# Strided heads as 18-token classes on four partition quarters, q and k cast in natural order, strided V cast in place, first two batches turned by TensorE

## The chip, the cores and the metric

The kernel runs on one core of one Trainium2 chip. The metric is device time in microseconds (us), from runs of the whole kernel; inputs and outputs lie in HBM. Engines are named as the profile names them: PE (TensorE; PEld its weight loads), DVE (VectorE), ACT (ScalarE), POOL (GpSimd), SP (SyncE). POOL and SP issue DMAs here; SPq in a row is an instruction that issues one on SP's hardware queue.

## The reference, cut to what matters

q, k and v are float32 [8 batches, 8 heads, 576 tokens, 64]. Heads 0 to 3 are local (a token sees itself and the 31 before it), heads 4 to 7 strided (a token sees the tokens before it, and itself, whose position has the same remainder by 32: 18 tokens for each of 32 remainders, a "class").

```python
    scores = scale * np.matmul(q, k.transpose(0, 1, 3, 2))
    mask_local = (rel >= 0) & (rel < stride)
    mask_strided = (rel >= 0) & (pos[None, :] % stride == pos[:, None] % stride)
...
    attn = attn / (np.sum(attn, axis=-1, keepdims=True) + 1e-09)
    return np.matmul(attn, v).astype(np.float32)
...
    h = x @ w_in
    P = a[0] + a[1] * h + a[2] * h2 + a[3] * h3
    Q = 1.0 + np.abs(b[0]) * np.abs(h) + np.abs(b[1]) * h2
    g = P / (Q + 1e-06)
    return (g @ w_out).astype(np.float32)
```

The attention output, tokens by 512 features (4608 rows), is x; w_in is 512 by 2048, w_out 2048 by 512, the output 4608 by 512 in float32.

## The kernel before, in words

All work is written as operations of a small planner (`Prog`). Each operation has an engine, an estimated duration, a key (its due time) and the tiles it reads and writes. `schedule` (L124) plays them through: on each engine the ready operation with the smallest key goes next. The result is one fixed order per engine, which the chip keeps; `emit` puts a semaphore wait ahead of each operation that needs one. So an operation that waits holds everything behind it on its engine, DMA issues on SP and POOL included. A DMA's estimate is a pair: the time that it takes of one common DMA resource, and a latency behind it (L185 to L188).

Per batch there are five steps.

1. `casts` (L419): POOL issues seven DMAs that read float32 from HBM and write bf16 back to HBM. Four of them (`local`, L428) interleave two local heads of q or k token by token, in runs of 64 elements (128 bytes), 1152 runs each; three (`bulk`, L436) copy strided q, strided k and all of v in natural order, in long runs.
2. `loads` (L463): SP issues four DMA transposes into SBUF (`lqT`, `lkT` L469; `sqT`, `skT` L475), each of 1152 rows of 128 elements (256 bytes); six DMAs for the local v tile `vL` (L481, L486: 4 x 64 x 17 + 2 x 64 = 4480 runs of 128 bytes), whose 32-token blocks lie on partitions twice over; eight DMAs for the strided v tile `vS` (L495: 8 x 36 x 16 = 4608 runs of 128 bytes).
3. `attention`: local scores in PSUM (L522, mask L509, row maximum on DVE L546, its subtraction by a matmul L553, exp on ACT L559 and L563), the probabilities turned by a DMA transpose (`ptL`, L566), their product with `vL` (L635), whose 65th column of ones gives the row sums, and a normalising multiply on DVE (`norm`, L655, L658). The strided heads go in two passes of two heads. Tokens are taken 36 at a time (remainder by 16, two classes in one; even and odd tokens on two partition halves), 64 products of 36 by 36 a batch (L591), with a mask that cuts the pairs apart; their probabilities are turned by two DMA transposes (`ptS`, L619), multiplied with `vS` (L687) and normalised.
4. The result is stored to HBM (`xs`; L665, L669, L696) and read back by DMA transposes into `xt`, features on partitions (`gather`, L711).
5. `mlp` works on chunks of 512 tokens (nine; chunk c can start when batch c is gathered, chunks 7 and 8 both need batch 7). In each, 16 blocks of four matmuls with `Win` (L731), a copy to bf16 on ACT (L735), then the rational function in two groups of 8 blocks: |h| on ACT (L746; for chunk 0 on DVE, L750), the denominator and the polynomial on DVE (L753, L755, L768 to L776), 1/Q as Ln and Exp on ACT (L759, L764). Then 64 matmuls with `Wout` (L789), four copies (L795) and four stores (L801).

The weights are cast into SBUF by four POOL DMAs between the casts of batches 0 and 1 and behind them. Casts of batch b+2 are tied to the first load of batch b+1. Attention of batch b has due times from `b*PER - 20`, gather `b*PER - 2`, its chunk `b*PER + 10`, with `PER` = 33.

## Time and profile before

| what | value |
|---|---|
| three timed runs | 584.54, 588.31, 590.23 us; median 588.31 us |
| profiled execution: span from first to last instruction | 586.6 us |
| busy: PE, DVE, ACT, POOL | 349.3, 314.7, 306.6, 61.5 us |
| mean granted TensorE clock | 0.903 of full speed |
| DMA packets, of which under 512 bytes | 213187, 196128 |
| first matmul with `Win` | at 152.61 us |

The span is that of one execution; the median of the timed runs is 1.7 us above it, and no separate time of the profiled execution is on the page. A row such as `L731 PE MATMUL ps<-xt,Win ... x554 | 149.1, 408 | 58.7 <-DMA xt<-xs 52.8` says: 554 matmuls of line 731, 149.1 us in which at least one of them ran, 408 ns from start to end of one (they overlap), and 58.7 us in which PE stood idle ahead of them, 52.8 of these until the DMA that fills `xt` had landed. In the rows of stretches the columns are length, busy time (and instructions) of PE, PEld, DVE, ACT and POOL, granted clock, the summed time of DMA packets as a share of 16 engines (over 1 where packets of two queues overlap), and GB/s.

### The profile page before, as it was taken

Reading aid. Unit: us, or ns where it says so; the run is one execution under the profiler, and the core shown is the slowest. Engines: PE = TensorE matmul, PEld = TensorE weight load, DVE = VectorE, ACT = ScalarE, POOL = GpSimd, SP = SyncE. Lnnn points to the kernel's source line nnn. Section 1 sums busy time; section 2 is a strip of 40 time slices with the busy share of each in tenths; the row PEclk is TensorE's granted clock in tenths of the full one; section 3 lists DMA queues with packets and bytes.
Section 4 is the critical chain, followed back from the end, with each engine's and each line's share of the span. In section 5 each row is a group of like instructions: output and inputs, shape, how many; then the busy total and the mean of one; then the engine's idle time right before and its main releaser. Section 6 shows DMA issues by size and latency. Waiting matters only on the chain.

```text
span 586.6 us, 7831 instructions
## 1 busy us (share of the span) xinstructions
PE 349.3 (60%) x3393; PEld 167.0 (28%) x3440; DVE 314.7 (54%) x227; ACT 306.6 (52%) x317; POOL 61.5 (10%) x64
## 2 busy tenths in 40 slices
PE   1012105103552379087796597994898899996846
...
DMA  9999999979999999979959995795214414000101
GB/s 127 182 163 121 91 114 172 73 145 174 82 133 185 61 153 165 87 114 181 127 86 200 115 100 123 142 103 127 46 45 97 71 39 115 19 36 18 54 19 72
DMA packets 213187, 62.71 MB, mean 107 GB/s; under 512 B 196128, under 2 KB 207008, under 8 KB 212640
## 3 DMA queue, kind: packets, MB, share of 16 engines
q1 hardware_dynamic: 171744, 43.84, 57.2%
q0 software_dynamic: 41408, 18.35, 27.8%
...
q14 instruction: 8, 0.07, 0.0%
HBM read 46.18 MB, written 28.31 MB: 127 GB/s over the span
## 4 chain that ended last, share of the span: by engine, by line
SPq 37%; PE 16%; DVE 16%; ACT 16%; DMA 12%; issue 4%; POOL 0%; ACTq 0%; POOLq 0%
SPq L495 10%; SPq L486 8%; PE ps L731 8%; PE ps L789 6%; DMA xt<-xs 5%; ACT z L746 5%; SPq L481 5%; DMA xs<-xS 4%; SPq L469 4%; SPq L475 4%; ACT h L735 4%; ACT u L759 3%; DVE u L755 3%; ACT u L764 2%; DVE z L770 2%
## 5 line engine op out<-in xcount | busy, mean ns | idle before, releaser
L731 PE MATMUL ps<-xt,Win 128*128 128x512 bf16 x554 | 149.1, 408 | 58.7 <-DMA xt<-xs 52.8
L789 PE MATMUL ps<-Wout,h 128*128 128x512 bf16 x553 | 149.9, 409 | 29.4 <-DVE h L776 17.0
L735 ACT ACTIVATE h<-ps 128x512 bf16<-128x512 f32 x144 | 82.0, 610 | 99.3 <-PE ps L731 98.4
L731 PEld LDWEIGHTS ps<-xt,Win 128*128 128x128 bf16 x576 | 56.3, 104 | 133.2 <-DMA xt<-xs 48.6
L789 PEld LDWEIGHTS ps<-Wout,h 128*128 128x128 bf16 x576 | 57.0, 104 | 101.5 <-DVE h L776 19.5
L759 ACT ACTIVATE u<-u,consts 128x2048 bf16<-128x2048 bf16 x36 | 70.6, 2000 | 19.3 <-DVE u L755 19.3
L764 ACT ACTIVATE u<-u 128x2048 bf16<-128x2048 bf16 x36 | 67.0, 1910 | 0.0
L428 POOL DMA_DIRECT2D lq<-in_q_dram x16 | 34.3, 2278 | 259.2 <-DMA lqT<-lq 258.4
L546 DVE TENSOR_REDUCE ng<-ps 128x18 bf16<-128x1152 f32 x8 | 10.8, 1356 | 93.5 <-PE ps L522 93.4
L746 ACT ACTIVATE z<-h 128x2048 bf16<-128x2048 bf16 x32 | 59.5, 1915 | 0.3
L522 PE MATMUL ps<-lkT,lqT 64*32 64x64 bf16 (+1 forms) x576 | 8.1, 207 | 79.6 <-DMA lkT<-lk 79.4
L753 DVE TENSOR_SCALAR u<-z,coef 128x4096 bf16<-128x4096 bf16 x18 | 24.1, 1338 | 58.2 <-ACT z L746 58.2
L559 ACT ACTIVATE pL<-ps 128x1024 bf16<-128x1024 f32 x8 | 8.2, 1019 | 79.9 <-PE ps L553 79.9
L776 DVE TENSOR_TENSOR h<-z,u 128x4096 bf16<-128x4096 bf16 x18 | 41.3, 2292 | 8.1 <-ACT u L764 7.6
L428 POOL DMA_DIRECT2D lk<-in_k_dram x16 | 41.6, 2923 | 0.0
L773 DVE TENSOR_TENSOR z<-z,h 128x4096 bf16<-128x4096 bf16 x18 | 41.2, 2291 | 0.5
L755 DVE TENSOR_TENSOR u<-u,z 128x4096 bf16<-128x4096 bf16 x18 | 41.1, 2283 | 0.4
L770 DVE TENSOR_TENSOR z<-z,h 128x4096 bf16<-128x4096 bf16 x18 | 40.9, 2272 | 0.3
L591 PE MATMUL ps<-skT,sqT 64*36 64x36 bf16 x512 | 20.2, 245 | 25.1 <-DMA skT<-sk 25.1
L795 ACT ACTIVATE os<-ps 128x512 f32<-128x512 f32 x36 | 21.5, 604 | 22.3 <-PE ps L789 22.2
L601 DVE TENSOR_REDUCE ng<-ps 100x16 bf16<-100x576 f32 x16 | 12.1, 755 | 35.8 <-PE ps L591 35.8
L522 PEld LDWEIGHTS ps<-lkT,lqT 64*32 64x32 bf16 x576 | 6.0, 94 | 86.9 <-DMA lkT<-lk 81.0
...
## 6 DMA issues: line engine op xcount, KB each, us to landing
...
```

What stands on the lines that cost most here:

```text
L428: P.op("pool", lambda e: e.dma_start(d_t[b, pair, :, :].rearrange("s (hh d) -> s hh d", hh=2), s_t[b, 2 * pair:2 * pair + 2, :, :].rearran ...
L486: P.op("sp", lambda e, hh=hh, pair=pair: e.dma_start(vl.t[64 * hh:64 * hh + 64, pair, 1:NB, 0:64], bass.AP(tensor=vs, offset=(b * H + 2 * ...
L495: P.op("sp", lambda e, r=r, h=h: e.dma_start(vS.t[64 * r:64 * r + CS, h, :, 0:64], bass.AP(tensor=vs, offset=(b * H + HL + h) * S * D, ap= ...
L731: r = e.matmul(bank(ph, 0, CH), Win[:, kk, f * 128:(f + 1) * 128], xt.t[:, kk, :], start=(kk == 0), stop=(kk == NK1 - 1))
L735: P.op("act", lambda e, f=f, ph=ph, h=h: e.activation(h.t[:, f % G, :], bank(ph, 0, CH), AF.Copy), 0.597, ky, r=[ph], w=[h], occ=0.494)
L746: P.op("act", lambda e, z=z, h=h, i=i: e.activation(z.t[:, half * i:half * i + half, :], h.t[:, half * i:half * i + half, :], AF.Abs), 1.9 ...
L755: dv(lambda e, z=z, u=u: e.tensor_tensor(u.t[:, :, :], u.t[:, :, :], z.t[:, :, :], op=Alu.mult), 2.28, 4, r=[z], m=[u])
L759: lns.append(P.op("act", lambda e, u=u, i=i: e.activation(u.t[:, half * i:half * i + half, :], u.t[:, half * i:half * i + half, :], AF.Ln, ...
L764: exs.append(P.op("act", lambda e, u=u, i=i: e.activation(u.t[:, half * i:half * i + half, :], u.t[:, half * i:half * i + half, :], AF.Exp ...
L770: dv(lambda e, z=z, h=h: e.tensor_tensor(z.t[:, :, :], z.t[:, :, :], h.t[:, :, :], op=Alu.mult), 2.28, 8, r=[h], m=[z])
L776: dv(lambda e, z=z, h=h, u=u: e.tensor_tensor(h.t[:, :, :], z.t[:, :, :], u.t[:, :, :], op=Alu.mult), 2.28, 14, r=[z, u], m=[h])
L789: r = e.matmul(bank(po, 0, Fout), groups[g].t[:, j, m * 128:(m + 1) * 128], Wout[:, kk, :], start=(kk == 0), stop=(kk == NF - 1))
```

## The change

Names stay; line numbers below are those of the changed file.

**Planner.** The DMA estimate has two queues, hardware (SP) and software (POOL), which share the engines; most durations and keys are new. Attention of batch b has due times from `b*35 - 26`, gather `b*35 - 8`, its chunk `b*35 + 10`. The rings of `xt` (2 to 3), `xl` and `xS` (1 to 2) grow, that of `h` shrinks (5 to 4 tiles).

**Casts.** No interleaving is left. For batches 2 to 7 there are five DMAs in long runs (local q and k, strided q and k, local v; 16 rows of 9216 elements each), into one HBM tensor `qk`. For batches 0 and 1, q and k go straight into SBUF (`sg`: 72 partitions with 8 tokens of each of 4 heads), and never through HBM. In every batch, strided v is cast straight into `vS` by four DMAs (18 partitions, runs of 512 elements), which takes its loads off SP.

```diff
-        local(0, q, lq, T_lq[b])
-        local(0, k, lk, T_lk[b])
-        local(1, q, lq, T_lq[b])
-        local(1, k, lk, T_lk[b])
-        bulk(q, sq, HL, HL, HL, T_sq[b])
-        bulk(k, sk, HL, HL, HL, T_sk[b])
-        bulk(v, vs, 0, H, H, T_v[b])
+            bulk(q, HL, qk, o + 2 * HS, T_qs[b])
+            bulk(k, HL, qk, o + 3 * HS, T_ks[b])
+            bulk(q, 0, qk, o, T_ql[b])
+            bulk(k, 0, qk, o + HS, T_kl[b])
+            bulk(v, 0, vs, b * HS, T_v[b])
+        t = R_vS.next()
+        for bq in range(4):
+            P.op("pool", lambda e, bq=bq, t=t: e.dma_start(
+                t.t[32 * bq:32 * bq + NI, :, :, :].rearrange("p h c d -> p h (c d)"),
+                bass.AP(tensor=v.tensor, offset=v.offset + (b * H + HL) * S * D + 8 * bq * D,
+                        ap=[[32 * D, NI], [S * D, HL], [1, 8 * D]])),
```

**Loads.** For batches 2 to 7, one DMA transpose brings strided q and k together (144 rows of 2048 elements, that is 2304 rows of 128), and one each local q and k (2304 rows of 128 elements that start 64 elements apart, so that a head lies on either partition half). `vL` is loaded once (4 DMAs, 2304 runs of 128 bytes) and its shifted second half copied inside SBUF (2 DMAs).

```diff
+            P.op("sp", lambda e, t=t: e.dma_start_transpose(
+                t.t[:, :, :], bass.AP(tensor=qk, offset=o + 2 * HS, ap=[[2048, 2 * HL * NI], [1, 2048]])),
+                1.4, key, r=[T_qs[b], T_ks[b]], w=[t], dma=(2.6, 2.0))
+            for nm, R, off, T in (("lq", R_lq, 0, [T_ql[b], T_kl[b]]), ("lk", R_lk, HS, [T_kl[b], T_qs[b]])):
...
+                    t.t[:, :], bass.AP(tensor=qk, offset=o + off, ap=[[D, HL * S], [1, 128]])),
+                    1.4, key + 0.1, r=T, w=[t], dma=(2.6, 2.0))
...
+            P.op("sp", lambda e, hh=hh: e.dma_start(
+                vl.t[64 * hh:64 * hh + 32, :, 1:NB, :], vl.t[64 * hh + 32:64 * hh + 64, :, 0:NB - 1, :]),
+                0.5, key + 0.3, r=[own], w=[vl], dma=(0.15, 2.0))
```

**Turning by PE.** For batches 0 and 1 PE transposes q and k (`turn_qk`, 128 small transposes, 8 copies shared by DVE and ACT), the probabilities (`turn`, 17 transposes, 4 copies), and the tokens of x that go into the batch's own chunk (`turn_x`, 24 transposes, 6 copies). Only their remaining 64 and 128 tokens go by `xs` and a gather. From batch 2 on the probabilities and x are turned by DMA as before, with one `ptS` transpose in the place of two.

**Strided heads.** 128 products of 18 by 18 a batch, four classes at a time on the four 32-partition quarters, all four heads in one pass: one mask (2 matmuls instead of 4), one maximum, one subtraction and one exp instead of two. The column of ones is gone from `vS`; row sums come from 8 matmuls with a 4-column block matrix `BO` and one reciprocal. The product with `vS` is 128 matmuls of 18 by 32 by 64 (L750), and two multiplies of 1024 columns stand for four DVE operations.

```diff
+                    for a in range(4):
+                        for p in range(2):
+                            c2 = 4 * bq + a
+                            r = e.matmul(bank(SS, 512 * p + NI * (4 * h + bq), NI, 32 * a, 32 * a + NI),
+                                         sqk.t[64 * p:64 * p + 64, c2, NI * h:NI * h + NI],
+                                         sqk.t[64 * p:64 * p + 64, c2, NI * (HL + h):NI * (HL + h) + NI],
+                                         start=False, stop=True, skip_group_check=True,
+                                         tile_position=(64 * p, 32 * a))
```

**MLP.** The groups are [4, 4, 8] blocks in chunk 0, [8, 4, 2, 2] in chunk 8, [8, 8] else. The second half of a chunk's `Wout` matmuls waits for its last group. Operations and their work are else the same.

```diff
+            sizes = [4, 4, 8] if nxt == 0 else [8, 4, 2, 2] if nxt == NCH - 1 else [8, 8]
+            mlp(nxt, nxt * PER + 10, sizes, [nxt > 0] * len(sizes))
```

**How the order moves.** First POOL, at the program's start. Before (`lq`, `lk`, `sq`, `sk`, `v` are HBM tensors):

```order
L428 DMA lq<-in_q_dram 1152x1x64
L428 DMA lk<-in_k_dram 1152x1x64
...
L436 DMA sq<-in_q_dram 16x9216
L436 DMA sk<-in_k_dram 16x9216
L436 DMA v<-in_v_dram 32x9216
L451 DMA Win<-in_moe_w_in_dram 128x4x1024 x2
```

Now (`sg` and `vS` lie in SBUF):

```order
L431 DMA v<-in_v_dram 16x9216
L441 DMA sg<-in_q_dram 72x4x512
L441 DMA sg<-in_k_dram 72x4x512
...
L454 DMA vS<-in_v_dram 18x4x512 x4
L464 DMA Win<-in_moe_w_in_dram 128x4x1024 x2
```

The two `L428` rows stand twice before, the two `L441` rows twice now: the first batch's nine DMAs stand ahead of `Win`, where seven stood.

Then PE, up to the first matmuls with `Win`. Before, the end of that stretch (batch 1's scores, then batch 0's local products, then chunk 0):

```order
L591 MATMUL ps<-skT,sqT 36x36 x64
L553 MATMUL ps<-ng,IDN 128x512 x2
L553 MATMUL ps<-ng,IDN 128x128
L608 MATMUL ps<-ng,IDN 100x288 x4
L635 MATMUL ps<-vL,ptL 32x65 x36
L731 MATMUL ps<-xt,Win 128x512 x36
L635 MATMUL ps<-vL,ptL 32x65 x36
L731 MATMUL ps<-xt,Win 128x512 x12
```

Now the same place (L571, L853 and L836 are transposes by PE; `sg` in L537 is batch 1's staged q and k):

```order
L571 MATMUL ps<-IDN,pL 128x128 x9
L734 MATMUL ps<-BO,ptS 128x4 x8
L750 MATMUL ps<-vS,ptS 32x64 x128
L783 MATMUL ps<-vL,ptL 32x65 x72
L853 MATMUL ps<-IDN,xS 128x128 x16
L836 MATMUL ps<-IDN,xl 128x128 x8
L889 MATMUL ps<-xt,Win 128x512 x16
L537 MATMUL ps<-IDN,sg 64x72 x128
```

Chunk 0 stands now behind one batch's attention instead of behind two batches' scores, and after its first 16 matmuls PE turns to batch 1's q and k.

Last SP, for one batch in the middle. Before (batch 2's loads, batch 0's gather between them):

```order
L469 DMA_TRANSPOSE lqT<-lq 128x2x576
L469 DMA_TRANSPOSE lkT<-lk 128x2x576
L475 DMA_TRANSPOSE sqT<-sq 128x4x288
L475 DMA_TRANSPOSE skT<-sk 128x4x288
L481 DMA vL<-v 32x2x64
L486 DMA vL<-v 64x17x64 x2
...
L711 DMA_TRANSPOSE xt<-xs 128x4x512
L711 DMA_TRANSPOSE xt<-xs 128x4x64
L495 DMA vS<-v 36x16x64 x8
L566 DMA_TRANSPOSE ptL<-pL 128x9x128
```

Now (batch 3's loads, with batch 2's stores and gather between them; two rows of `out_dram` stores left out):

```order
L485 DMA_TRANSPOSE sqkT<-qk 128x16x144
L765 DMA xs<-xS 72x2x256 x4
L491 DMA_TRANSPOSE lqT<-qk 128x2304
L491 DMA_TRANSPOSE lkT<-qk 128x2304
L500 DMA vL<-v 32x18x64 x4
...
L808 DMA xs<-xl 128x4x256
L817 DMA xs<-xl 64x128 x2
...
L514 DMA vL<-vL 32x2x1105 x2
L561 DMA_TRANSPOSE ptS<-pS 128x8x128
L870 DMA_TRANSPOSE xt<-xs 128x4x384
```

The eight `vS` rows are gone from SP, and batch 2's gather stands behind batch 3's `ptS`, which needs batch 3's scores.

More of the change, by code (lines that the diff above doesn't have):

```diff
@@ L623, in attention, with srcL, ssum @@
-        key += 14
+        def srcL():
+            return ppL.t
+        srcL.tile = ppL
+        turn(srcL, ptL, 9, key, 1.3)
+        T_xs[b].new()
+        t0 = b * S
+        key += 8
+        SB_ = Banks(1)
+        def ssum(e):
+            r = None
+            for g in range(8):
+                r = e.matmul(bank(SB_, 4 * g, 4), ptS.t[:, g, :], BO[:, :], start=True, stop=True, skip_group_check=True)
+            return r
+        P.op("pe", ssum, 8 * 0.07, key, r=[ptS, T_c], w=[SB_])
+        rcS = R_rc.next()
```

657 lines of the change are left out of this document (390 added, 267 removed).

## The prediction

> **What bounds the kernel now.** I read the page's slices first, then the stretches between gathers, then SP's queue, then the groups of instructions.
>
> ```profile
> PE   1012105103552379087796597994898899996846
> DMA  9999999979999999979959995795214414000101
> q1 hardware_dynamic: 171744, 43.84, 57.2%
> q0 software_dynamic: 41408, 18.35, 27.8%
> GB/s 127 182 163 121 91 114 172 73 145 174 82 133 185 61 153 165 87 114 181 127 86 200 115 100 123 142 103 127 46 45 97 71 39 115 19 36 18 54 19 72
> ```
>
> The DMA engines are full for two thirds of the span while PE is nearly idle for a quarter and half used up to the middle; only the last third looks like a compute kernel. The stretches below run from one gather, or one batch's first load, to the next:
>
> ```profile
> 83.20:125.60 42.40, 10.77 (x285) 7.35 (x286) 7.07 (x9) 2.27 (x4) 6.94 (x7) 1.00 1.20 133
> 164.50:208.70 44.20, 13.86 (x230) 7.19 (x230) 36.19 (x27) 18.11 (x14) 7.43 (x7) 0.63 1.25 132
> 365.20:407.20 42.00, 32.02 (x324) 14.85 (x329) 25.64 (x19) 28.19 (x31) 0.00 (x0) 0.87 0.84 123
> 407.20:449.20 42.00, 37.46 (x409) 17.77 (x415) 34.50 (x25) 34.14 (x35) 0.00 (x0) 0.95 0.31 74
> 449.20:492.00 42.80, 39.72 (x344) 19.03 (x351) 34.08 (x26) 35.28 (x37) 0.00 (x0) 0.92 0.30 68
> ```
>
> Up to 208 us packets overlap on all engines (share over 1) and compute waits: 42 to 44 us a batch is what the DMA engines need for casts and loads. From 365 us the casts are over, from 407 us the loads too (share 0.3), and PE, DVE and ACT are 80 to 93% busy; a batch still takes 42 us. How SP stands in the full part, and where chunk 0, chunk 7 and the end lie:
>
> ```profile
> 20.04 9.98 SPq L475 DMA_TRANSPOSE sqT<-sq  x1
> 386.10 10.56 SPq L495 DMA_DIRECT2D vS<-v  x8
> 152.61 9.25 PE L731 MATMUL ps<-xt,Win 128*128 128x512 bf16 x35 [10.21 <-DMA xt<-xs]
> 491.93 7.07 PE L731 MATMUL ps<-xt,Win 128*128 128x512 bf16 x31
> 573.76 9.62 PE L789 MATMUL ps<-Wout,h 128*128 128x512 bf16 x32 [9.81 <-DVE h L776]
> ```
>
> So the 586.6 us are three pieces: 152.6 to the first MLP matmul, 339.3 (to 491.9) for seven steps of a chunk, 48.5 each, and 94.7 for chunk 6's rest, chunks 7 and 8 and the drain. I cost the change in the same three pieces.
>
> **The start: 152.6 becomes 36, and 6 of a stall.** Removed from the way to chunk 0 are the HBM round trip of q and k, four load transposes, eight `vS` DMAs, three probability transposes, and batch 1's scores, ahead of which its loads had to come. What is left begins with POOL:
>
> ```profile
> 1.29 1.48 POOL lq L428
> 2.98 5.91 DMA lq<-in_q_dram
> L436 POOL DMA_DIRECT2D sq<-in_q_dram x8: 2780/2824/5158, 4.5 to 317.1; - x8
> DMA to landing us min/median/max: 3.5/9.1/39.8
> L451 POOL DMA_DIRECT2D Win<-in_moe_w_in_dram x2: 3108/3132/3157, 6.0 to 6.8; - x2
> DMA to landing us min/median/max: 17.3/19.8/22.4
> 32.57 0.91 PE L522 MATMUL ps<-lkT,lqT 64*32 64x64 bf16 x72 [26.67 <-DMA lkT<-lk]
> 38.33 0.27 ACT L563 ACTIVATE pL<-ps 128x128 bf16<-128x128 f32 x1
> ```
>
> The first cast lands at 8.9 us (second row; the landing figures belong to the row above each). Five DMAs stand now before q and k are staged, 1.4 MB in bf16 in long runs; between the first landing of one (8.9) and that of `Win` behind 2 MB more (6 + 20 = 26) I take 16. Then one chain: last transposes and copies 2, scores, maximum, subtraction and exp 6 (before, the local ones took from 32.57 to 38.60, last two rows), turning 2, products and multiplies 6, turning x 2: 34. `vS` and `Win` land by 20 and 30, hidden behind the chain. I take 36; bounds 28 (everything lands in 10 us) and 50 (`Win` last, after nine casts). Behind 16 matmuls PE meets batch 1's transposes, as the order shows. Their casts are issued behind `Win`, at about 10 us; before, the longest landing of a `sq` cast was 39.8 us, which from there ends at 50. With fewer short runs ahead I put it at 46, against 39.5 for PE (36 and 16 matmuls at 0.216): a stall of 6, bounds 0 and 14; queued behind it on PE are the rest of chunk 0, and for them wait ACT's copies. The turning work of batch 1 (8 copies of some 0.7 us and 10 of 0.6 shared by DVE and ACT, by the 0.61 of line 735 for 512 columns, about 6 us on each) is hidden in this stall and chunk 0's thin start; without that cover it costs 6 more. Batch 0's is in the chain.
>
> **The steady part: 48.5 becomes 38.5.** First DMA, since it sets the pace now. Packet time per batch: loads (0.84 - 0.31) x 42.0 = 22.3 us for 4480 + 4608 + 4608 = 13,696 packets, 26 ns each on 16 engines; the round trip of probabilities and x 0.30 x 42 = 12.6; casts, 27.8% of 586.6 less the weights in eight parts, or directly from one batch:
>
> ```profile
> q0 software_dynamic: 4784, 1.77, 42.8%
> ```
>
> (queues in the stretch 83.2 to 125.6) 0.428 x 42.4 = 18.1. Together 53, in a wall time of 42 to 44 by the overlap of 1.25. Now: 4608 cast runs of 128 bytes become 64 long and 288 middling ones. The bytes stay; the nearest row for long runs is `Win` (2 MB in about 20 us, beside all else), which puts the 1.8 MB at 18 at worst; the page's best slice, 200 GB/s, puts them at 9. I take 12, nearer to the best, since 4608 of the 4784 packets of those 18.1 were short ones. Loads: 2304 runs for `vL` instead of 9088 for both v tiles, but 2304 x 3 = 6912 transposed rows instead of 4608: 9216 x 26 ns / 16 = 15, and 1 for the copy inside SBUF. Round trip 12.6. Sum 40.6 of packet time, 32.5 on the wall by the same overlap; with the cast at its worst and no overlap 46.6.
>
> A rule speaks against the transposes. Local q and k rows start 128 bytes apart, so that every second one begins at an odd multiple of 128; the Trainium skill, DMA: Bandwidth & Descriptors, section How a descriptor splits into AXI transactions, says that a descriptor off a 256-byte start fetches from the boundary below it. By its way of counting 256 bytes then cost 12 beats instead of 8; as an estimate from it, 4608 of the rows would cost a quarter more, about 2 us a batch, and the sum would be 42.6. No row of before has such a start, so the trace cannot say.
>
> Next the engines, per batch, from these groups:
>
> ```profile
> L759 ACT ACTIVATE u<-u,consts 128x2048 bf16<-128x2048 bf16 x36 | 70.6, 2000 | 19.3 <-DVE u L755 19.3
> L746 ACT ACTIVATE z<-h 128x2048 bf16<-128x2048 bf16 x32 | 59.5, 1915 | 0.3
> L735 ACT ACTIVATE h<-ps 128x512 bf16<-128x512 f32 x144 | 82.0, 610 | 99.3 <-PE ps L731 98.4
> L764 ACT ACTIVATE u<-u 128x2048 bf16<-128x2048 bf16 x36 | 67.0, 1910 | 0.0
> L795 ACT ACTIVATE os<-ps 128x512 f32<-128x512 f32 x36 | 21.5, 604 | 22.3 <-PE ps L789 22.2
> L755 DVE TENSOR_TENSOR u<-u,z 128x4096 bf16<-128x4096 bf16 x18 | 41.1, 2283 | 0.4
> L768 DVE TENSOR_SCALAR z<-h,coef 128x4096 bf16<-128x4096 bf16 x18 | 23.9, 1325 | 0.3
> L546 DVE TENSOR_REDUCE ng<-ps 128x18 bf16<-128x1152 f32 x8 | 10.8, 1356 | 93.5 <-PE ps L522 93.4
> L658 DVE TENSOR_TENSOR xS<-ps,rc 100x1152 bf16<-100x1152 f32 (+1 forms) x16 | 19.3, 1217 | 0.0
> L601 DVE TENSOR_REDUCE ng<-ps 100x16 bf16<-100x576 f32 x16 | 12.1, 755 | 35.8 <-PE ps L591 35.8
> L614 ACT ACTIVATE pS<-ps 100x576 bf16<-100x576 f32 x16 | 10.4, 666 | 20.3 <-PE ps L608 20.3
> L578 PE MATMUL ps<-MS,IDN 128*128 128x288 bf16 x32 | 8.0, 345 | 2.6 <-ACT pL L563 0.8 <-DVE xS L658 0.8 <-ACT os L795 0.7
> L608 PE MATMUL ps<-ng,IDN 100*100 100x288 bf16 x32 | 7.9, 351 | 1.8 <-DVE ng L601 1.8
> L591 PE MATMUL ps<-skT,sqT 64*36 64x36 bf16 x512 | 20.2, 245 | 25.1 <-DMA skT<-sk 25.1
> L522 PE MATMUL ps<-lkT,lqT 64*32 64x64 bf16 (+1 forms) x576 | 8.1, 207 | 79.6 <-DMA lkT<-lk 79.4
> L687 PE MATMUL ps<-vS,ptS 36*64 36x65 bf16 (+1 forms) x512 | 13.6, 217 | 16.0 <-DMA ptS<-pS 8.4 <-issue 7.1 <-ACT pS L614 0.4
> ```
>
> PE: 128 MLP matmuls at 0.216 ((7.07 - 0.38) / 31 in the row at 491.93) are 27.7. Strided scores: 128 at between 14 ns (8.1/576, products in 32-column tiles) and 39 (20.2/512), 1.8 to 5.0; the new ones are such tiles, 1.8, where before paid 2.5. The product with `vS`: 128 at 15 to 27 ns, 1.9 against 1.7. Masks and subtraction for strided heads halve (15.9 / 8 becomes 1.0), row sums add 0.6, and the local part keeps its 4. So attention on PE takes about 9, and PE needs 37 at full clock. ACT: 9.1 + 7.8 + 7.4 + 7.7 + 2.4 for a chunk (82.0, 70.6, 67.0 and 21.5 over nine; 4 x 1.915), 2 for attention (one exp of 0.67 gone): 36. DVE: 28.8 for 16 wide operations (four of 2.28 and four of 1.32 a group), 6.7 for attention (1.36 and 0.76 for the maxima, 1.35 + 2 x 1.22 for the products, three reciprocals), one maximum less than before: 35.5. All three stand at 35 to 37, above DMA's 32.5. Before, with DMA out of the way, the same work took 42.0 to 42.8, 4 to 9 us of that PE waiting for `xt`: attention was due 14 us before its gather's chunk needed it. Now it is due 18 us ahead of the gather and 36 ahead of the chunk, and no tile of x blocks the next (rings of 3 and 2), so this wait should go, and what shows instead is the queueing between three engines of equal load. Batch 2's gather waits on SP behind batch 3's `ptS`; behind that stand `xt` and so PE's next chunk, hidden as long as batch 3's loads come a chunk ahead. Floor 36, ceiling 42.5 (before's own); I take 38.5 as PE at 0.95 of the clock, the value of the stretch at 407.
>
> On the clock: it was 0.63 where PE worked 13.9 of 44.2 us and 0.95 where it worked 37 of 42. The Trainium skill, TensorE: Matmul & The Clock Gate, section What's actually happening, has the clock at half after about 3.4 us of idleness and at full otherwise; the trace agrees in direction. By that rule a PE that never waits would run at 1.0, and seven steps would be some 11 us shorter.
>
> **The end: 94.7 becomes 85.** Chunk 6's second group, chunks 7 and 8 keep their work, about 17 us a group. The drain shrinks: the last group's last product ends at 573.7, and 32 matmuls, copies and stores follow to 586.6, 12.9 us. With a last group of 2 blocks only 8 matmuls (1.7) wait for it, 6 us with copy and store; and the group's own chain over DVE and ACT is a quarter as wide, worth some 3 more. The extra instructions (two more groups) cost ACT and DVE about 1 us, hidden in that chain's waits.
>
> Sum: 36 + 6 + 7 x 38.5 + 85 = 396.5 against the profiled 586.6. The median of the runs stands 1.7 above that span, so I predict **398 us**.
>
> **Rivals.**
> - *DMA keeps the pace.* Share 1.25 up to 208 us speaks for it, the 32.5 us on the wall against. With 45 us a batch for six batches and a stall of 14: 36 + 14 + 6 x 45 + 38.5 + 85 + 1.7 = 445. Chance 0.22.
> - *The engines pack to their floor*, with the clock full: 36 + 7 x 36 + 82 + 1.7 = 372. For it: the last groups of before follow each other at 17 us; against: three engines of equal load, each handing to the next. Chance 0.17.
> - *Slower.* The overlapping rows at 128-byte starts and the 36 KB runs make the new loads dear: DMA transposes of 6912 rows on the one SP queue, behind which gather, `ptS` and stores stand. It decides from (588.3 - 36 - 6 - 38.5 - 85 - 1.7) / 6 = 70 us a batch on. For that the 6912 rows, 11 us at 26 ns, would have to cost some 4 times as much. The row at 20.04, where one transpose took 9.98 of the queue beside casts, shows that they can be slowed so, but only beside full queues. At 75 us a batch: 617. Chance 0.03.
> - *Nothing gained*: the wait moves from loads to another chain of the same length, some 70 us a batch as there, within 1%: chance 0.02.
>
> **How the numbers follow.** My forecast (380 to 425 around 398) has 0.56, DMA's pace 0.22, the floor 0.17, the others 0.05. The range 370 to 445 leaves out the tails of the first two rivals beyond their prices and the slow cases, about 0.2. About 1% is what a measurement of this kernel can tell from no change: faster by more than that 0.95, within 0.02, slower 0.03.
>
> **What would show it.** In the changed profile: first matmul on `xt` and `Win` near 36 us; q0's packets down by 30,000; DMA share under 1 in stretches after 100 us; no `vS` on SPq; chunk starts 36 to 42 us apart; ACT, DVE and PE each above 85% between 100 us and the drain; the last `Wout` run of about 8 matmuls. I am wrong if chunk starts stand 45 apart with PE waiting for DMA (`sqkT`, `xt`), or if chunk 0 begins after 50.

## The result, and the profile after

| | before | changed | predicted |
|---|---|---|---|
| median of the timed runs | 587.67 us (584.54 to 590.23) | 450.31 us (443.02 to 458.94) | 398 us (370 to 445) |
| ratio to before, 95% interval | | 0.757 [0.749, 0.764] | |
| profiled execution, span | 586.6 | 441.2 | 396.5 |
| start, to the first `Win` matmul | 152.6 | 49.5 | 36 |
| seven steps, to chunk 7's first `Win` matmul | 339.3 | 299.3 | 269.5, and 6 of a stall |
| chunk 7's start to the end | 94.7 | 92.4 | 85 |

The change is faster, as forecast, by much less than forecast: 45 us of the profiled time are missing: 13.5 in the start, 24 in the steps (the stall counted in), 7 in the end. The ratio 0.757 on 587.67 us is 445 us, the upper edge of the range; the median of all four runs lies beyond it. Executions of one kernel differ by up to 5% here (443 to 459 us for the change), so the ratios go by the faster executions alone, and the pieces of flat copies, no turning, |h| on DVE in the tail and free casts, whose profiles are slower executions, can be some 10 us too long.

Page of the changed kernel:

```profile
span 441.2 us, 10622 instructions
PE 339.6 (77%) x4782; PEld 166.9 (38%) x4834; DVE 331.8 (75%) x252; ACT 323.4 (73%) x337; POOL 48.0 (11%) x80
DMA  7999997288999999997998999332224011010012
q0 software_dynamic: 11968, 18.37, 25.4%
L889 PE MATMUL ps<-xt,Win 128*128 128x512 bf16 x558 | 146.5, 403 | 13.1 <-DMA xt<-xs 7.9
```

q0's packets fell by 29,440 (41,408 before), as predicted. No engine is full: PE, DVE and ACT are 77, 75 and 73% busy. Where each piece ends is read by counting weight loads; the first row is of line 889 alone (stretch, length, PE, PEld, clock, DMA share, GB/s), the others of all lines (columns as in the rows of stretches ahead of the prediction):

```profile
0.00:348.70 348.70, 116.47 (x431) 43.41 (x449) 0.92 0.89 145
49.50:348.70 299.20, 246.64 (x3875) 120.76 (x3918) 238.65 (x173) 230.25 (x242) 28.21 (x45) 0.90 0.82 142
348.70:441.20 92.50, 75.34 (x323) 32.51 (x327) 74.74 (x57) 79.26 (x83) 0.00 (x0) 0.93 0.12 43
```

Seven chunks are 448 weight loads; the 449th stands just ahead of a `Win` matmul at 348.78, so chunk 7 starts there. In the seven steps the busiest engine, PE, works 246.6 of 299.2 us (82%), DVE 80, ACT 77. From 100 us to the drain each was forecast above 85%; from 100 to 420 us they are 83, 81 and 82%. DMA share is 0.82 over the steps, but not under 1 in every stretch after 100 us, as I had forecast: from 127 to 193 us it is 1.10 to 1.13. Chunk starts stand 42.8 us apart in the mean and 34 to 56 singly, where I had forecast 36 to 42; chunk 0 begins at 49.5, just ahead of the 50 that I had named as a sign of being wrong.

The start, PE and SP in time order (idle before in brackets):

```profile
9.00 1.17 PE L537 MATMUL ps<-IDN,sg 72*64 72x72 bf16 x32 [9.00 <-DMA sg<-in_q_dram]
39.64 0.30 PE L750 MATMUL ps<-vS,ptS 18*32 18x64 bf16 x15 [6.37 <-issue]
43.32 1.43 PE L783 MATMUL ps<-vL,ptL 64*32 64x65 bf16 x72 [3.38 <-DMA vL<-v]
49.49 4.97 PE L889 MATMUL ps<-xt,Win 128*128 128x512 bf16 x15 [1.93 <-ACT xt L843]
5.86 5.57 SPq L500 DMA_DIRECT2D vL<-v  x4
11.47 19.59 SPq L508 DMA_DIRECT2D vL<-v  x4
```

The first of the four casts of q and k into `sg` lands at 9.0, the last at 16.2, as the 16 that I took; `vS` is in by 19.3 and `Win` by 28.9, ahead of their 20 and 30. But the eight `vL` loads of batch 0 hold SP until 31.1 and land at 43.2, and PE had stopped for 6.4 us already ahead of that with no wait shown. `vL` was in none of the chain's terms.

For that stop the trace has a candidate. One of the two DMA queues that the page names `instruction`, q8, moves 38 packets of 16,384 bytes. One of these runs from 36.75 to 38.15 us, and PE goes on at 39.64, 1.5 us behind it. PE's two shorter stops without a shown wait, ahead of 24.96 and 31.16, end 1.5 and 1.6 us behind the two packets before. In all eleven runs that turn batches 0 and 1 by PE, the change among them, the stop at the product with `vS` lasts 5.0 to 6.6 us and ends 1.4 to 2.2 us behind such a packet. By this timing PE seems to have waited for its own instructions, beside full DMA queues; no run moved those packets, so that is not tested.

One step in the middle, POOL, SP and PE:

```profile
203.64 0.53 POOL L431 DMA_DIRECT2D qk<-in_q_dram  x1 [27.92 <-DMA vL<-vL]
209.95 9.04 SPq L485 DMA_TRANSPOSE sqkT<-qk  x1
222.31 2.66 SPq L870 DMA_TRANSPOSE xt<-xs  x2
225.70 1.04 PE L889 MATMUL ps<-xt,Win 128*128 128x512 bf16 x4 [3.48 <-DMA xt<-xs]
```

POOL's casts wait until the loads of the batch before have landed; `sqkT` is issued beside them and holds SP for 9 us; the gather of batch 4 stands behind it; PE waits 3.5 us for it. In the group row over the whole run (`L889` on the page above) PE's wait for `xt` is 7.9 us, where it was 52.8. And DVE, where the polynomial is, with ACT in the same time:

```profile
228.27 1.29 DVE L939 TENSOR_SCALAR z<-z,coef 128x4096 bf16<-128x4096 bf16 x1
235.39 0.36 DVE L738 RECIPROCAL rc<-ps 128x32 f32<-128x32 f32 x1 [5.83 <-PE ps L734]
235.67 2.23 DVE L941 TENSOR_TENSOR h<-z,u 128x4096 bf16<-128x4096 bf16 x1
226.77 0.60 ACT L893 ACTIVATE h<-ps 128x512 bf16<-128x512 f32 x1 [2.73 <-PE ps L889]
231.17 3.70 ACT L927 ACTIVATE u<-u 128x2048 bf16<-128x2048 bf16 x2
```

L941 ends a group and lets PE go on with `Wout`. It needs L939's result, ready at 229.6, and `u`, the exp of L927 on ACT, ready at 234.9. It runs at 235.7. The attention operation L738, whose sums (L734) come late, was ordered ahead of it, but that costs only 0.8 us here: what is late is the exp, which stands on ACT behind the copies L893 of the next chunk, and the first of these waited for PE, which waited for the gather. So one late gather passes from PE to ACT to DVE. (In the other groups L941 runs at most 1.4 us after both its inputs are there.) Three kinds of loss are thus in the trace: a late start, transposes beside casts, and waits of three engines, each idle for about a fifth of the steps, on each other. The experiments weigh them.

### The profile page after: what moved, and what is told of

It is laid out like the page before. It is cut to its first block, busy times and chain, and to the rows that moved or that the text cites. A ratio compares the mean times of both kernels' runs of the same rounds, so it can differ in the third digit from the quotient of the medians.

```text
span 441.2 us, 10622 instructions
## 1 busy us (share of the span) xinstructions
PE 339.6 (77%) x4782; PEld 166.9 (38%) x4834; DVE 331.8 (75%) x252; ACT 323.4 (73%) x337; POOL 48.0 (11%) x80
## 4 chain that ended last, share of the span: by engine, by line
ACT 32%; PE 30%; DMA 12%; SPq 11%; DVE 9%; issue 5%; POOL 0%; ACTq 0%; POOLq 0%
PE ps L889 15%; ACT u L922 9%; PE ps L957 9%; ACT u L927 8%; ACT h L893 6%; ACT z L909 6%; DMA vL<-v 4%; SPq L508 4%; DMA xt<-xs 4%; SPq L500 2%; SPq L491 2%; SPq L485 2%; ACT os L965 2%; DVE u L918 2%; PE ps L783 1%
## 5 line engine op out<-in xcount | busy, mean ns | idle before, releaser
L889 PE MATMUL ps<-xt,Win 128*128 128x512 bf16 x558 | 146.5, 403 | 13.1 <-DMA xt<-xs 7.9
L893 ACT ACTIVATE h<-ps 128x512 bf16<-128x512 f32 x144 | 81.5, 610 | 50.4 <-PE ps L889 50.3
L889 PEld LDWEIGHTS ps<-xt,Win 128*128 128x128 bf16 x576 | 55.8, 102 | 83.7 <-issue 12.6
L922 ACT ACTIVATE u<-u,consts 128x2048 bf16<-128x2048 bf16 (+1 forms) x40 | 71.4, 1830 | 3.2 <-DVE u L918 3.2
L927 ACT ACTIVATE u<-u 128x2048 bf16<-128x2048 bf16 (+1 forms) x40 | 67.6, 1737 | 0.1
L909 ACT ACTIVATE z<-h 128x2048 bf16<-128x2048 bf16 (+1 forms) x34 | 60.2, 1822 | 2.0 <-DVE h L941 1.7
L916 DVE TENSOR_SCALAR u<-z,coef 128x4096 bf16<-128x4096 bf16 (+2 forms) x21 | 25.1, 1195 | 25.0 <-ACT z L909 25.0
L918 DVE TENSOR_TENSOR u<-u,z 128x4096 bf16<-128x4096 bf16 (+2 forms) x21 | 41.9, 1996 | 0.6
L937 DVE TENSOR_TENSOR z<-z,h 128x4096 bf16<-128x4096 bf16 (+2 forms) x21 | 41.7, 1985 | 0.5
L933 DVE TENSOR_TENSOR z<-z,h 128x4096 bf16<-128x4096 bf16 (+2 forms) x21 | 41.6, 1983 | 0.5
L941 DVE TENSOR_TENSOR h<-z,u 128x4096 bf16<-128x4096 bf16 (+2 forms) x21 | 41.6, 1979 | 0.4
L537 PE MATMUL ps<-IDN,sg 72*64 72x72 bf16 x256 | 8.4, 238 | 22.4 <-DMA sg<-in_q_dram 9.0
L931 DVE TENSOR_SCALAR z<-h,coef 128x4096 bf16<-128x4096 bf16 (+2 forms) x21 | 24.8, 1181 | 0.5
L757 DVE TENSOR_TENSOR xS<-ps,rc 128x1024 bf16<-128x1024 f32 x16 | 19.3, 1220 | 7.6 <-PE ps L750 7.6
L935 DVE TENSOR_SCALAR z<-z,coef 128x4096 bf16<-128x4096 bf16 (+2 forms) x21 | 23.7, 1127 | 0.4
L939 DVE TENSOR_SCALAR z<-z,coef 128x4096 bf16<-128x4096 bf16 (+2 forms) x21 | 23.6, 1123 | 0.5
L454 POOL DMA_DIRECT2D vS<-in_v_dram x32 | 21.2, 674 | 11.6 <-PE ps L750 11.6
L750 PE MATMUL ps<-vS,ptS 18*32 18x64 bf16 x1024 | 10.9, 209 | 12.9 <-issue 8.0
```

Of the source, the lines that this page charges most:

```text
L889: r = e.matmul(bank(ph, 0, CH), Win[:, kk, f * 128:(f + 1) * 128], xt.t[:, kk, :], start=(kk == 0), stop=(kk == NK1 - 1))
L893: P.op("act", lambda e, f=f, ph=ph, h=h, f0=f0: e.activation(h.t[:, f - f0, :], bank(ph, 0, CH), AF.Copy), 0.6, ky, r=[ph], w=[h], occ=0.48)
L909: P.op("act", lambda e, z=z, h=h, i=i, hp=hp: e.activation(z.t[:, hp * i:hp * i + hp, :], h.t[:, hp * i:hp * i + hp, :], AF.Abs), dact, ky ...
L916: dv(lambda e, z=z, u=u, G_=G_: e.tensor_scalar(u.t[:, 0:G_, :], z.t[:, 0:G_, :], b1_ap, b0_ap, op0=Alu.mult, op1=Alu.add), True, 2, r=[z, ...
L918: dv(lambda e, z=z, u=u, G_=G_: e.tensor_tensor(u.t[:, 0:G_, :], u.t[:, 0:G_, :], z.t[:, 0:G_, :], op=Alu.mult), False, 4, r=[z], m=[u])
L922: lns.append(P.op("act", lambda e, u=u, i=i, hp=hp: e.activation(u.t[:, hp * i:hp * i + hp, :], u.t[:, hp * i:hp * i + hp, :], AF.Ln, bias ...
```

## The experiments

A table first: ratios are to the kernel before on the same chip; the last three columns are the pieces of each profiled execution. The last row has no ratio on record.

| run | median us (lowest to highest) | ratio to before [95%] | start | steps | end |
|---|---|---|---|---|---|
| the change | 450.31 (443.02 to 458.94) | 0.757 [0.749, 0.764] | 49.5 | 299.3 | 92.4 |
| small casts | 430.78 (426.63 to 431.37) | 0.730 [0.724, 0.736] | 50.3 | 286.6 | 92.5 |
| light DMA | 431.20 (430.01 to 434.67) | 0.736 [0.731, 0.741] | 49.7 | 287.4 | 92.6 |
| short runs | 479.86 (474.26 to 482.08) | 0.813 [0.805, 0.822] | 54.7 | 330.7 | 92.6 |
| free casts | 458.42 (451.35 to 461.00) | 0.774 [0.760, 0.788] | 49.3 | 315.6 | 92.7 |
| `vL` by copy in all batches | 452.24 (447.73 to 456.96) | 0.765 [0.757, 0.773] | 46.6 | 310.5 | 91.7 |
| flat copies | 444.35 (442.58 to 452.86) | 0.757 [0.752, 0.761] | 48.0 | 311.0 | 92.1 |
| `Wout` held | 458.16 (453.85 to 458.66) | 0.779 [0.772, 0.786] | 48.9 | 314.7 | 92.4 |
| no turning by PE | 486.07 (478.80 to 490.13) | 0.816 [0.807, 0.824] | 88.0 | 308.6 | 91.4 |
| \|h\| on DVE in the tail | 448.15 (442.71 to 452.30) | 0.755 [0.746, 0.763] | 49.9 | 310.1 | 88.2 |
| half of \|h\| on DVE | 421.15 (419.55 to 427.91) | 0.717 [0.712, 0.722] | 48.4 | 282.3 | 87.0 |
| the same, order kept | 447.11 (441.76 to 462.06) | | 50.1 | 302.5 | 89.5 |

### What of the gain came from where

Before, without its `vS` loads:

```diff
-        vS = R_vS.next()
+        vS = R_vS.next() if b < 2 else R_vS.tiles[b % 2]
...
-        for r in range(2):
+        for r in range(2 if b < 2 else 0):
```

> The kernel before; from batch 2 on the eight loads of strided v into vS are left out (the tiles keep what batches 0 and 1 brought, so the strided product of the later batches is not computed from their own v). If the DMA queue on SP kept the pace before, as the prediction has it, 48 DMAs fewer shorten each of batches 2 to 5 by some 8 us and the whole from 588 to 535-555. Rival: the loads were hidden behind other waits, and the whole stays above 575.

Measured: 546.11 us in one run, beside 586.57 for the kernel before: 40 us less for 48 DMAs. Stretches from gather to gather of this run:

```profile
324.50:363.70 39.20, 37.41 (x417) 18.11 (x422) 34.50 (x26) 34.30 (x37) 0.00 (x0) 1.00 0.75 122
363.70:402.60 38.90, 36.20 (x408) 17.53 (x414) 34.56 (x26) 34.49 (x37) 0.00 (x0) 1.00 0.31 78
```

The DMA queue did keep the pace before; with it lightened the kernel before runs these two stretches, in which its casts are over, in 39 us each, with PE 93 to 95% busy. So my 38.5 was in reach of these engines there; over all its seven steps this run still took 41.6 us a step (290.9 in all), and its first `Win` matmul came at 158.6. The run lightens SP's queue and the DMA engines at once and does not tell them apart.

The change, with the first two batches by DMA:

```diff
-    NPE = 2
+    NPE = 0
```

> No batch is turned by TensorE: batches 0 and 1 go through HBM and DMA transposes like the others. If the turning buys the short start, the first matmul with Win comes at 65 to 80 us and the time is 20 to 35 us longer (465 to 480); if its slow copies (2.7 us each, 8 of them, on DVE and ACT) eat the gain, the time stays within 8 us of 445.

Measured: 486.07, 36 us above the change. The first `Win` matmul comes at 88.0, later than the 65 to 80 expected. Turning by PE gives the start 38 of its 103 us, and these come through to the end.

### The start

`vL` in the first two batches by four loads and two copies, as in the others:

```diff
-            if b < NPE:
+            if b < 0:
...
-        if b < NPE:
-            vl.w = list(own.w)
```

> Batches 0 and 1 get the shifted half of the local v tile by two copies inside SBUF, as the later batches do, in the place of four more loads in runs of 128 bytes. If vL's landing at 43 us is what holds chunk 0 back, chunk 0 starts at 38 to 44 instead of 49.5, and the whole is 5 to 10 us shorter; if the strided products (their second part at 39.6 us) hold it as well, it starts at 46 to 48 and the whole moves by under 4.

```profile
37.89 0.30 PE L748 MATMUL ps<-vS,ptS 18*32 18x64 bf16 x15 [5.27 <-issue]
40.82 1.43 PE L781 MATMUL ps<-vL,ptL 64*32 64x65 bf16 x72 [2.62 <-DMA vL<-vL]
```

Chunk 0 comes 2.9 us earlier, at 46.6, as expected if `vL` does not hold it alone; PE's stop stays. The whole does not gain; the planner made another order for it, and its steps are longer in this profile.

The strided copies of the first two batches written in a row (tokens in another order there):

```diff
-                        o_ = dst.t[:, S * pair:S * pair + S].rearrange("p (t j) -> p j t", j=8)
+                        o_ = dst.t[:, S * pair:S * pair + S].rearrange("p (j t) -> p j t", j=8)
...
-                    o_ = xt.t[:, 2 + hp, c0:].rearrange("p (i b a r) -> p b a i r", i=ni, b=4, a=4)[:, :, :, :, r_]
+                    o_ = xt.t[:, 2 + hp, c0:].rearrange("p (r b a i) -> p b a i r", i=ni, b=4, a=4)[:, :, :, :, r_]
```

> The change with the copies of the first two batches (lqT, lkT, sqkT out of PSUM, and xS into xt) written in a row instead of with a stride; the order of tokens in these batches is then another one, so their output is not the reference's. Same instructions and order. If the strided copies of 2.7 us are on the start's chain: the copies take 0.65-0.75 us, the first Win matmul comes 3-6 us earlier (44-46 us), batch 1's stall shrinks by some 4 us, the whole 440-446. Rival: the start waits on vL's landing and PE's own stall, the first Win matmul stays after 47.5 and the whole moves by less than 1%.

Line 553 of the change (min/median/max ns), then PE of this run:

```profile
L553 ACT ACTIVATE lqT<-ps x2: 2712/2712/2712, 11.5 to 55.6; 128x576 bf16<-128x576 bf16 x2
L553 DVE COPY sqkT<-ps x4: 740/754/759, 19.2 to 65.2; 128x576 bf16<-128x576 bf16 x4
```

```profile
42.70 1.43 PE L783 MATMUL ps<-vL,ptL 64*32 64x65 bf16 x72 [5.20 <-DMA vL<-v]
48.03 5.62 PE L889 MATMUL ps<-xt,Win 128*128 128x512 bf16 x15 [1.09 <-ACT xt L843]
53.58 0.45 PE L537 MATMUL ps<-IDN,sg 72*64 72x72 bf16 x16
58.01 0.57 PE L537 MATMUL ps<-IDN,sg 72*64 72x72 bf16 x16 [0.68 <-DVE sqkT L553]
```

The local copies cost 2.7 us, not my 0.7, and 0.45 (DVE) or 0.65 (ACT) without the stride. Yet batch 0's chain gains only 1.5 us: it meets `vL`, whose wait grows from 3.4 to 5.2. Batch 1's turn takes 5.0 us (53.6 to 58.6) instead of 9.6 (54.4 to 64.0), as expected, and the timed ratio does not move (0.757). What became of the 6 us that the two save together is not shown.

The casts of `Wout` and of batch 2 held until batch 0's `vL` has landed, order kept:

```diff
-    P.schedule()
+    P.schedule(); T_wout[0].w[0].deps.update({d: 1 for d in vl0})
```

(`vl0` are batch 0's eight `vL` loads.)

> The change, the casts of Wout and of batch 2 held until the vL loads of batch 0 have landed; same order on every engine. Theory, that vL's landing at 43 us and PE's stall of 6.4 us ahead of it come from the casts queued beside them: vL of batch 0 lands by 38, PE's stall shrinks under 4 us, the first Win matmul comes at 41-45 us, whole 442-448. Rival, that the casts of batch 1 and Win (issued before 22 us) are enough to hold vL up, or its short runs themselves take that long: the first Win matmul stays after 47 us and the whole is within 1% or later.

```profile
42.89 1.43 PE L783 MATMUL ps<-vL,ptL 64*32 64x65 bf16 x72 [2.95 <-DMA vL<-v]
43.04 1.80 POOL L471 DMA_DIRECT2D Wout<-in_moe_w_out_dram  x2 [18.57 <-DMA vL<-v]
```

The rival holds: with 18.6 us of POOL's queue empty of new casts, `vL` lands at 42.9 all the same and PE's stop stays at 6.6. What holds `vL` up is older than 24 us (the casts of batch 1 or `Win`) or the loads' own short runs. No run parts these cleanly; the run with copies points to the casts, since with half of the short runs gone `vL` was still in only at 40.7, and its two copies inside SBUF took 7.6 and 7.7 us to land, where those of later batches took 2.6 in the median. The hold itself costs 15 us in the steps; the held casts now run in the first of them.

### DMA in the steps

Small casts from batch 3 on: rows of 512 elements instead of 9216, and the loads read batch 2's data (so later batches compute on that):

```diff
-                bass.AP(tensor=d_t, offset=off, ap=[[n, 16], [1, n]]),
+                bass.AP(tensor=d_t, offset=off, ap=[[n, 16], [1, m_]]),
```

> Leaves out most of the casting of q, k and local v from batch 3 on (each of these casts moves 512 of 9216 elements a row), and loads batch 2's q, k and v again; every instruction, wait and order stays. Theory A (the steady part at 41 us a chunk is set by long cast runs that slow SP's transposes, behind which the gathers stand): the sqkT transposes fall from 8 to 9 us on SP's queue to 2 to 4, batch 4's gather comes 6 to 10 us earlier, the time falls from about 445 to 418 to 428. Theory B (the fixed order couples three engines of equal load, DMA hides): sqkT falls as well, but the time stays above 436.

`sqkT` in the change, then here (min/median/max ns of SP's time, first and last start):

```profile
L485 SPq DMA_TRANSPOSE sqkT<-qk x6: 2256/6951/9039, 67.5 to 246.3; - x6
```

```profile
L485 SPq DMA_TRANSPOSE sqkT<-qk x6: 2315/2712/4089, 66.1 to 240.1; - x6
```

The transposes drop to 2.7 us, and the steps by 13 us; chunk steps stay at 41. Nearer to the theory of casts in the way, but it leaves 11 of the missing 24 us, and the whole end.

Light DMA: the same, and from batch 4 on the three transposes bring 16 of 144 and 128 of 2304 rows:

```diff
-                t.t[:, :, :], bass.AP(tensor=qk, offset=o + 2 * HS, ap=[[2048, 2 * HL * NI], [1, 2048]])),
+                (t.t[:, :, :] if b < 4 else t.t[:, :, 0:16]), bass.AP(tensor=qk, offset=o + 2 * HS, ap=[[2048, 2 * HL * NI if b < 4 else 16], [1, 2048]])),
```

> The change with nearly no DMA work of casts and loads in the later batches: casts from batch 3 on move 512 of 9216 elements a row, the three q and k transposes from batch 4 on bring 16 of 144 and 128 of 2304 rows, vL and vS read batch 2's data (so those batches compute on other data). Same order on every engine. Theory A, DMA is the rest of the pace: below 415 us, steps of 35-36 us. Theory B, what is left after the small casts is the coupling of PE, DVE and ACT in their fixed order: 422-432, within 2% of the small casts alone (430.8), and groups of the polynomial still end 19-20 us apart until the last gather.

```profile
DMA  7999999096899755544653585231233101000012
```

The DMA engines are half idle from the middle on, and the time is that of the small casts: 431.2 against 430.8. Casts and loads thus cost some 12 us of the 24 in the steps (12 to 16 by the timed ratios). The round trips of probabilities and x through DMA stay in this run, but no engine of PE, DVE and ACT waits for one of them for 2 us in all: the rest is not DMA.

Short runs: each cast in 64 runs of 2304 elements, nothing left out:

```diff
-                bass.AP(tensor=d_t, offset=off, ap=[[n, 16], [1, n]]),
+                bass.AP(tensor=d_t, offset=off, ap=[[n // 4, 4], [n, 16], [1, n // 4]]),
```

> The change, its casts into HBM cut into 64 runs of 2304 elements in the place of 16 of 9216 that can be merged; same bytes, same order on every engine. Theory A, that the long runs of the casts hold up the transposes beside them: the sqkT transposes fall from 8-9 us to 3-6, the gathers of batches 2 to 6 come some 2 us a step earlier, 432-442 us (ratio to before 0.735-0.75). Theory B, that the step is set by the engines' order and not by transposes: within 1% of the change, 446-454. A third: that only bytes count, and transposes stay at 8 us whatever the length of the runs.

Landing times of the casts, the change and this run, and `sqkT` here:

```profile
qk<-in_q_dram POOLq DMA_DIRECT2D x12, 288.0 KB, 6.7
```

```profile
qk<-in_q_dram POOLq DMA_DIRECT2D x12, 288.0 KB, 11.6
```

```profile
L485 SPq DMA_TRANSPOSE sqkT<-qk x6: 3261/6522/10035, 66.9 to 285.4; - x6
```

None of the three foresaw the time: the transposes stay near 7 us, as the third had it, but the casts land 5 us later and 30 us are lost. The theory that long runs hold up the transposes falls; what is left is the casts' work beside them, and short runs make that work longer.

Free casts, not held until the loads before have landed, order kept:

```diff
-    P.schedule()
+    P.schedule(); [o.deps.pop(d, None) for o in P.ops for d in o.soft]
```

(`soft` are the loads that a cast is held for.)

> The change, the casts of later batches no longer held until the loads of the batch before have landed; same order on every engine, the casts of batch b+2 then go as soon as those of b+1 and the strided product of batch b-1 let POOL go on. Theory A, a serial loop (loads landed, casts, transposes, gather behind them): the sqkT transposes find their data there and the casts out of the way, they take 2-5 us, the gather of batch 4 is in before 218, whole 432-442. Rival, bytes: the casts only collide with the loads of the batch before in the place of their own, transposes stay at 6-9 us somewhere, whole 445-455.

```profile
42.29 0.55 POOL L431 DMA_DIRECT2D qk<-in_q_dram  x1
58.23 12.68 SPq L508 DMA_DIRECT2D vL<-v  x4
```

The casts of batch 3 now go at 42.3 instead of 99.8 us, and batch 1's second `vL` loads hold SP for 12.7 us. The transposes do get cheap, as theory A had it (`sqkT` 3.4 us in the median, 7.0 in the change), and still nothing is gained: 0.774 against 0.757, with overlapping intervals. So neither the serial loop nor the slow transposes by themselves are the loss; that the same bytes collide elsewhere, as the `vL` row shows in one place (6.65 us there in the change), is the likely reason.

### The engines

|h| on DVE in chunks 6 to 8:

```diff
-            mlp(nxt, nxt * PER + 10, sizes, [nxt > 0] * len(sizes))
+            mlp(nxt, nxt * PER + 10, sizes, [0 < nxt < 6] * len(sizes))
```

> In chunks 6 to 8 |h| is computed on DVE (about 1.2 us for 8 blocks) and not on ACT (3.8 us). If ACT alone paces the last 100 us (it is busy 49.5 of 49.5 us from 350 to 399.5), the groups there follow at 15 to 16 us instead of 16.3 to 17.4 and the time falls by 6 to 10 us; if DVE or PE stand as close behind, by under 3.

```profile
360.00:407.50 47.50, 43.54 (x201) 18.87 (x199) 46.54 (x28) 40.22 (x46) 0.00 (x0) 1.00 0.09 34
```

No measurable change of the time: DVE takes ACT's place, 46.5 of 47.5 us busy. The end piece is 4.2 us shorter in this profile, which the timed runs can't confirm.

Half of every |h| on DVE, with the planner's own order for it:

```diff
-                for i in range(npc):
-                    P.op("act", lambda e, z=z, h=h, i=i, hp=hp: e.activation(
-                        z.t[:, hp * i:hp * i + hp, :], h.t[:, hp * i:hp * i + hp, :], AF.Abs),
-                        dact, ky, r=[h], w=[z], occ=dact - 0.1)
+                P.op("act", lambda e, z=z, h=h, hp=hp: e.activation(
+                    z.t[:, 0:hp, :], h.t[:, 0:hp, :], AF.Abs), dact, ky, r=[h], w=[z], occ=dact - 0.1)
+                if npc > 1: P.op("dve", lambda e, z=z, h=h, hp=hp: e.tensor_scalar(
+                    z.t.bitcast(u16)[:, hp:2 * hp, :], h.t.bitcast(u16)[:, hp:2 * hp, :], 0x7FFF, None, op0=Alu.bitwise_and), 0.15 + hp * CH * 0.26e-3, ky, r=[h], w=[z])
```

> The change with the second half of each group's |h| on DVE (a bitwise and) in the place of ACT; the planner makes its own order for it. With light DMA the steps did not fall under 39 us, and the largest single wait of DVE is L916 waiting for ACT's |h| (24.6 us in all). Theory, that this hand-over ACT to DVE is the coupling that costs: ACT loses 30 us of work, DVE gains about 12, the L916 wait falls under 12 us, whole 436-445. Rival, that DVE is the next bound and every us taken from ACT is given back: L916's wait shrinks but DVE's busy time grows by as much, whole 446-456.

Measured: 421.15, better than either theory, with all DMA in place; by the ratios (0.717 against 0.757) and by the profiles (417.7 against 441.2) some 23 us under the change. It is the fastest of all. Groups of DVE in the change and here (busy, mean ns, idle before):

```profile
L916 DVE TENSOR_SCALAR u<-z,coef 128x4096 bf16<-128x4096 bf16 (+2 forms) x21 | 25.1, 1195 | 25.0 <-ACT z L909 25.0
L698 DVE TENSOR_REDUCE ng<-ps 128x18 bf16<-128x1152 f32 x8 | 10.8, 1356 | 11.6 <-PE ps L674 11.4
L738 DVE RECIPROCAL rc<-ps 128x32 f32<-128x32 f32 x8 | 2.8, 354 | 12.6 <-PE ps L734 12.6
```

```profile
L916 DVE TENSOR_SCALAR u<-z,coef 128x4096 bf16<-128x4096 bf16 (+2 forms) x21 | 25.1, 1193 | 4.5 <-ACT z L908 4.5
L738 DVE RECIPROCAL rc<-ps 128x32 f32<-128x32 f32 x8 | 2.8, 352 | 2.3 <-PE ps L734 2.3
```

Not only the wait for |h| goes (25.0 to 4.5); so does that of L738 for late attention sums (12.6 to 2.3), to which the edit does nothing but order. In time order, the place that was shown above:

```profile
232.72 2.29 DVE L941 TENSOR_TENSOR h<-z,u 128x4096 bf16<-128x4096 bf16 x1 [0.58 <-ACT u L927]
234.93 0.35 DVE L738 RECIPROCAL rc<-ps 128x32 f32<-128x32 f32 x1
```

Here L941 stands ahead of L738, and the exp is there at 232.7 instead of 234.9. So two causes remained, and the last run parts them: the same half on DVE right ahead of its user, every other operation where the change has it.

```diff
+    for o in P.ops:
+        if getattr(o, "alt", None):
+            u = [x for x in o.users if x.eng == "dve"]
+            P.order["act"].remove(o); o.eng, o.maker = "dve", o.alt
+            P.order["dve"].insert(min(P.order["dve"].index(x) for x in u), o)
```

> The change with the second half of each group's |h| on DVE, right ahead of the operation that uses it; nothing else moves (the half-|h| run of 421 us came with an order of its own from the planner). Theory, the hand-over itself costs: taking 1.8 us of ACT per group out of DVE's way is what gained, DVE's wait at L916 falls from 25 to under 12 us, whole 418-432. Rival, the planner's other order gained (two groups interleaved on DVE, so that a wait of one is covered by the other): with the old order DVE only works 11 us more and waits elsewhere, whole 438-450. Between these, 432-438, both count.

```profile
L916 DVE TENSOR_SCALAR u<-z,coef 128x4096 bf16<-128x4096 bf16 (+2 forms) x21 | 25.1, 1197 | 5.5 <-ACT z L909 5.1
L698 DVE TENSOR_REDUCE ng<-ps 128x18 bf16<-128x1152 f32 x8 | 10.8, 1356 | 16.0 <-PE ps L674 16.0
L738 DVE RECIPROCAL rc<-ps 128x32 f32<-128x32 f32 x8 | 2.8, 354 | 10.9 <-PE ps L734 10.9
```

Measured: 447.11 (the lowest run 441.76, that of the change 443.02). The wait for |h| goes as before (25.0 to 5.5) and nothing is gained: DVE has 10.2 us more to do (342.0 busy instead of 331.8), and waits longer for PE elsewhere (L698, 16.0 instead of 11.6). The theory of the hand-over falls, the rival holds: the other order of the same operations is what gained. Whether that order would gain as much with all of |h| on ACT was not tried.

Where it gained must be counted by something that the order does not pull forward. I take the 13th of the 21 polynomial groups, behind which attention is nearly over: it ends at 329.5 in the change and 321.8 in the half-|h| run. So 8 us are won up to there and 16 behind it, though the table, whose border is chunk 7's first `Win` matmul, puts 17 into the steps. From there to the end of the last group, in the change, with the order kept, and with the planner's order:

```profile
329.50:432.10 102.60, 89.96 (x390) 39.10 (x397) 89.27 (x66) 93.73 (x95) 0.00 (x0) 0.93 0.12 40
333.20:433.20 100.00, 89.13 (x393) 39.38 (x400) 92.82 (x72) 84.67 (x90) 0.00 (x0) 0.97 0.13 42
321.80:411.00 89.20, 78.74 (x358) 35.07 (x364) 87.76 (x69) 79.15 (x82) 0.00 (x0) 1.00 0.13 43
```

DMA is nearly at rest here (share 0.12 to 0.13). With the order kept DVE is 93% busy and the eight groups take 100 us; with the planner's they take 89, and DVE is 98% busy. In that order DVE works on two of these groups in turn, where the change finishes one and then waits for the next one's |h| (2.7 us at 352.61):

```profile
325.89 1.34 DVE L931 TENSOR_SCALAR z<-h,coef 128x4096 bf16<-128x4096 bf16 x1
327.15 1.34 DVE L916 TENSOR_SCALAR u<-z,coef 128x4096 bf16<-128x4096 bf16 x1
328.40 2.28 DVE L933 TENSOR_TENSOR z<-z,h 128x4096 bf16<-128x4096 bf16 x1
```

(L931 and L933 belong to one group, L916 to the next.) Up to the 13th group no group's L916 stands inside another group in either order, so the 8 us won there have another reason, which stays open.

## Why the prediction was right and wrong

- **Direction and mechanism: right.** The DMA queue kept the pace before, as the run without `vS` shows (40 us for 48 loads); the interleaving casts, the `vS` loads and most waits for `xt` are gone. The rival of dear overlapping transposes did not come. The Trainium skill's rule (DMA: Bandwidth & Descriptors, How a descriptor splits into AXI transactions) has a descriptor that starts off 256 bytes fetch from the boundary below, from which I had estimated a quarter more time. No run here shows that: with casts out of the way `lqT` and `lkT`, half of whose rows have such starts, land in a median of 5.5 and 5.8 us, `sqkT`, with as many rows and none, in 6.2.
- **The start, 36: failed at "products and multiplies 6".** The casts came as forecast (16.2, 19.3 and 28.9 for 16, 20 and 30). From 16.2 on the terms measured 5.3 for the last transposes and copies (2 taken), 7.5 for scores to exp (6), 3.1 for turning (2), 14.4 for products and multiplies (6) and 3.0 for turning x (2). In the 14.4 lie PE's stop of 6.4 us and the wait for `vL`, whose eight loads of short runs land at 43.2 and stood in no term. The copies, taken at 0.7 us from a row without a stride, cost 2.7 where they are strided; that alone is worth only 1.5 in the start.
- **The stall of 6: near by luck.** I had batch 1's casts land at 46, after PE was there. They landed by 40.4, and PE came to them only at 54.4. It left them at 64.0 all the same, with idle time of some 6 us in between, because it waited for the strided copies: without the stride this took 5.0 instead of 9.6 us.
- **The steps, 38.5: failed at "the wait should go, and what shows instead is the queueing between three engines of equal load", and at its price.** PE's wait for `xt` did nearly go (52.8 to 7.9), though one premise was misread: by the keys before, attention was due 18 us ahead of its gather and 30 ahead of its chunk, not 14; now it is 18 and 36. I gave the queueing 1.5 us over PE's 37 (38.5), as if it were only the clock. The step took 5.8 over it (42.8): some 0.9 of this is the stall, 1.7 the casts and loads (12 us over seven steps, light DMA), and some 3, by what is left, the waits of the engines on each other. A better order with half of |h| moved takes about 1 a step (8 us up to the 13th group). The gains need not add up. The time looks like the rival in which DMA keeps the pace (445), but for most of it that was not the cause: with DMA half idle the kernel still takes 431.
- **The end, 85: mis-sized by 7.** I took 6.9 off the drain and 3 off the last group's chain. The last group's last product ends at 432.1, 9.1 ahead of the end (12.9 before); from chunk 7's start to that product it is 83.3 us (81.8 before). The narrow last groups shortened no chain that set this stretch. The 17 us a group that I carried over held (16 to 17 for the wide ones); they came from the order, for with two groups in turn on DVE, and half of |h| there, the last eight took 89 instead of 103 us (100 with the order kept).
- **The clock.** I wrote that the trace agreed with the Trainium skill's rule in direction. That left out my own row at 83.20, where the clock was 1.00 though PE worked only 10.8 of 42.4 us. In the change it was 0.98 where PE worked 42.3 of 49.5 us (350 to 399.5), 0.90 over the steps, and 1.00 up to 49.5, where PE worked 17.7 us. The 0.98 fits the Trainium skill's rule (TensorE: Matmul & The Clock Gate, What's actually happening) that a PE which keeps busy has its full clock; that the clock falls to half after idleness, the row at 83.20 and the start do not show. Nor did the mean clock set the time: two executions of light DMA with 0.889 and 0.916 spanned 429.1 and 428.2 us.
